# Local attention normalised two steps behind its scores, weight splits held back behind named instructions, projections spread from step 16

## The chip, the core and the metric

The kernel runs on one core of a Trainium2 chip. The metric is the device time of one execution in microseconds. The core has five engines that each take their instructions in order: TensorE (PE; its weight loads are PEld), VectorE (DVE), ScalarE (ACT), GpSimd (POOL) and SyncE (SP), which only issues transfers.

## What is computed

Three layers, one after the other, on 4 batches of 512 local and 32 global rows each (576 in all later), with a width of 512.

```python
# 1 local + global attention, 8 heads of 64, window 32
s_g = scale * q_g @ concat(k_g, k_l).T;  out_g = softmax(s_g) @ concat(v_g, v_l)
s_l = concat(scale * q_l @ k_g.T, where(|i - j| <= 32, scale * q_l @ k_l.T, -1e9))
out_l = softmax(s_l) @ concat(v_g, v_l)
x = rows(concat(out_g, out_l))
# 2 four experts, causal attention, weighted by the two best of x @ w_gate
ye = softmax(causal(scale * (x @ wq[e]) @ (x @ wk[e]).T)) @ (x @ wv[e]) @ wo[e]
x = sum over e of gate_e * ye
# 3 MLP on x and the row before it
k = max((mu_k * x + (1 - mu_k) * x_prev) @ w_k, 0)
out = sigmoid((mu_r * x + (1 - mu_r) * x_prev) @ w_r) * ((k * k) @ w_v)
```

Products that need more than one pass of reduced precision are made of three: a tensor is split into a high part H and a low part L = x - H, and H H, L H and H L are summed (lines 93 to 95).

## The kernel before

**Stage A, local attention.** Thirty-two steps n, four to each of eight groups u. `a_qk` computes scores S on TensorE (L198), VectorE adds the mask `band` and takes the negative maximum (L208, mn), and ScalarE makes the exponentials in place (sm, L211, with their sums su). `a_norm` makes 1/su on VectorE (rc, L223 and 224) and multiplies on GpSimd (pn, L228, and glob, L231). `a_tp` transposes pn on TensorE (pT, L243) and copies it to pt. Once a group `g_qk`, `g_norm`, `g_tp` do the global rows (Sga, pg, mng, pTG), and `a_pv` multiplies by v (x, L311). In the loop over n, `a_norm` does step n-1 and `a_tp` step n-2. `ts` of step n and `pn` have three buffers each (`csm0`, `csm1`).

**Weights of the projections.** `load_wb(step)` issues the transfers of wq, wk or wv (rawwq, ...) at n = 4, 8, 12; `split_wb`, one chunk a step from the same step on, makes H on ScalarE (L154, behind the last exponential) and L on GpSimd (L155).

**Stage B and C, projections and experts.** `b_groups(b)` is a list of projection pieces of batch b; those of batch 0 are laid into steps n = 26 to 33, the others into `c_step`. `c_step(m)` runs 36 units and starts at n = 34: `c_qk` (scores C, csm), `c_norm` (crc; csm on GpSimd, L479), `c_tp` (cT, cpt) and `c_pv` (y), a step apart each; `wo_groups` makes po. The rows of x are cast to H by VectorE (L343).

**Weights of the MLP.** `load_wd` loads a chunk of w_k, w_v or w_r (raw data of 64-bit numbers, taken as pairs of 32-bit words) and splits it at once: Sign and Abs on ScalarE (L125, 126; wg, wy), a maximum on GpSimd (L127), a shift, an or and an xor on VectorE (L129 to 131), H on ScalarE (L132), L on GpSimd (L133). Chunks of w_k come at m = 8, 11, ..., four of w_v at m = 31, 33, 35, 37, the rest of w_v (4 to 7) and w_r behind the last unit.

**Stage D, the MLP.** Nine tiles of tokens. `d_mix` makes the mixed rows (mmr on VectorE, m0, m1 split by ScalarE and GpSimd, L634 and 635), `d_k` k (ksr, k2r, kk; the low part on GpSimd, L651), `d_v` v, `d_r` r, `d_out` the product and its store. For tile 0 TensorE needs all eight chunks of w_v.

**What sets the order.** The code is written as one stream; the framework then orders each engine's instructions by a timeline of its own. `tc.issue_after(i)` around an instruction keeps it behind i. A buffer of a tag is handed out again when its last reader is done.

## Time and profile before

| | us |
|---|---|
| median of 3 runs (lowest, highest) | 583.22 (581.43, 584.19) |
| profiled execution | 579.51 |
| its span | 577.7 |
| TensorE busy, idle in the span | 546.5, 31.2 |
| VectorE, ScalarE, GpSimd busy | 350.3, 330.8, 315.0 |
| granted clock of TensorE, mean | .982 |

The profile gives, for one execution, the busy time of each engine, the idle time before an instruction with the instruction that ended it (its releaser), and the clock that TensorE was granted (1.00 is full, .50 half). An idle time of TensorE is read by following its releaser back: to the engine that was late, and to what that one waited for.

### The profile page before, as it was taken

The page shows a single profiled execution, that of the slowest core. Times are in us where ns is not written, and L with a number is a line of the kernel's source. Part 1 is how long each engine was busy: PE and PEld are TensorE (multiplying, and loading weights), DVE is VectorE, ACT ScalarE, POOL GpSimd, SP SyncE. Part 2 cuts the span into 40 slices and gives each one's busy share as a digit, 9 for nine tenths or more (in the row PEclk, how much of TensorE's full clock was granted, in tenths as well). Part 3 has the DMA queues.
Part 4 walks back from the last instruction along what each step waited for, and adds up shares of the span by engine and source line. Part 5 has one row for each costly group of instructions (what it writes and reads, how often), then busy time and mean ns, then how long its engine had stood idle before and what let it go on. Part 6 is the DMA issues. An engine that isn't in the chain of part 4 may idle for free.

```text
span 577.7 us, 12767 instructions
## 1 busy us (share of the span) xinstructions
PE 546.5 (95%) x4670; PEld 456.8 (79%) x4670; DVE 350.3 (61%) x1145; ACT 330.8 (57%) x995; POOL 315.0 (55%) x416
## 2 busy tenths in 40 slices
PE   3879999999999999799899898999999999999997
PEld 2657767889987888588778786888898989898896
DVE  2545677468678668648788989969343343324211
ACT  3676777555546465347579667677444554434221
POOL 1755765465356546636567999967444444334120
PEclk9897999999999999799999999999999999999999
DMA  8974645023101101011111222010000000000000
GB/s 346 324 210 135 199 172 174 2 76 83 48 1 38 38 21 54 2 37 38 37 38 38 74 74 75 35 39 36 1 38 1 37 1 36 19 19 37 2 19 36
DMA packets 19775, 38.85 MB, mean 67 GB/s; under 512 B 9472, under 2 KB 10496, under 8 KB 19712
## 3 DMA queue, kind: packets, MB, share of 16 engines
q1 hardware_dynamic: 19136, 37.46, 19.9%
q8 instruction: 37, 0.61, 0.4%
q10 hardware_dynamic: 576, 0.57, 0.3%
q14 instruction: 26, 0.21, 0.1%
HBM read 33.57 MB, written 4.46 MB: 66 GB/s over the span
## 4 chain that ended last, share of the span: by engine, by line
PE 65%; DVE 13%; ACT 8%; POOL 5%; DMA 5%; issue 3%; SPq 1%; ACTq 0%; DVEq 0%; POOLq 0%
PE v L93 4%; PE v L94 4%; PE v L95 4%; PE k L94 4%; PE k L93 4%; PE k L95 4%; PE y L557 4%; PE cT L487 3%; PE C L101 3%; PE x L311 3%; PE r L93 2%; DVE x L343 2%; PE r L94 2%; PE r L95 2%; PE S L198 2%
## 5 line engine op out<-in xcount | busy, mean ns | idle before, releaser
L651 POOL TENSOR_TENSOR kk<-k2r,kk 128x256 fp32r<-128x256 f32 x64 | 50.6, 793 | 68.3 <-ACT kk L650 68.3
L648 DVE TENSOR_TENSOR k2r<-ksr 128x256 f32<-128x256 f32 x64 | 36.9, 578 | 70.5 <-ACT ksr L647 64.3
L479 POOL TENSOR_TENSOR csm<-csm,crc 128x128 f32<-128x128 f32 (+3 forms) x64 | 50.1, 803 | 47.3 <-DVE crc L476 22.6
L211 ACT ACTIVATE sm<-sm,mn 128x160 f32<-128x160 f32 x128 | 53.4, 419 | 23.4 <-DVE mn L208 23.1
L631 DVE SCALAR_TENSOR_TENSOR mmr<-xT,mu,mtr 128x256 f32<-128x256 f32 (+4 forms) x96 | 58.8, 648 | 10.7 <-POOL m L635 4.1
L228 POOL TENSOR_TENSOR pn<-sm,rc 128x256 f32<-128x256 f32 x64 | 38.0, 614 | 43.6 <-DVE rc L224 23.2
L463 ACT ACTIVATE csm<-csm,cmn 128x128 f32<-128x128 f32 (+3 forms) x64 | 35.8, 561 | 27.3 <-DVE cmn L461 27.3
L647 ACT ACTIVATE ksr<-k 128x256 f32<-128x256 f32 x64 | 24.1, 377 | 40.5 <-PE k L95 40.0
L630 ACT ACTIVATE mtr<-xT,omu 128x256 f32<-128x256 f32 (+4 forms) x96 | 40.3, 442 | 7.7 <-DVE mmr L631 7.0
L208 DVE CUSTOM_DVE_ANT_0 sm<-S,band 128x160 f32<-128x160 f32 x128 | 34.2, 320 | 16.9 <-DMA band<-in_band_dram 9.0
L635 POOL TENSOR_TENSOR m1L<-mmr,m1H 128x256 fp32r<-128x256 f32 (+1 forms) x36 | 27.6, 779 | 30.5 <-ACT m1H L634 30.4
L650 ACT CAST kk<-k2r 128x256 fp32r<-128x256 f32 x64 | 25.9, 404 | 25.7 <-DVE k2r L648 22.7
L198 PE MATMUL S<-kq 64*64 64x160 f32 x512 | 31.1, 325 | 7.6 <-DMA kq<-in_kq_dram 4.1
L557 PE MATMUL y<-cpt,vC 128*64 128x128 f32 (+1 forms) x320 | 35.8, 300 | 0.0
L461 DVE CUSTOM_DVE_ANT_0 csm<-C,causal 128x128 f32<-128x128 f32 (+3 forms) x64 | 29.7, 485 | 4.9 <-PE C L101 3.5
L696 DVE TENSOR_TENSOR o<-v,rt 128x512 f32<-128x512 f32 x17 | 11.6, 685 | 33.4 <-ACT m1H L634 18.2
L487 PE MATMUL cT<-ident,csm 128*128 128x128 f32 x160 | 27.0, 286 | 5.0 <-DVE cpt L492 2.4
L198 PEld LDWEIGHTS S<-kq 64*64 64x64 f32 x512 | 19.7, 140 | 15.1 <-issue 6.9
L311 PE MATMUL x<-pt,vw 128*64 128x64 f32 x512 | 30.6, 244 | 0.1
L243 PE MATMUL pT<-ident,pn 128*128 128x128 f32 x128 | 22.3, 300 | 8.1 <-DVE mng L274 4.0
L311 PEld LDWEIGHTS x<-pt,vw 128*64 128x64 f32 x512 | 25.9, 149 | 5.0 <-issue 3.9
L557 PEld LDWEIGHTS y<-cpt,vC 128*64 128x64 f32 x320 | 21.7, 137 | 9.1 <-issue 5.7
(408 smaller groups left out, 1894.7 us busy)
## 6 DMA issues: line engine op xcount, KB each, us to landing
kq<-in_kq_dram SPq DMA_DIRECT2D x15, 688.0 KB, 5.5
...
```

The lines of the kernel that those rows point to most:

```text
L93: nc.tensor.matmul(o, wH, xH, start=start, stop=False)
L94: nc.tensor.matmul(o, wH, xL, start=False, stop=False)
L95: nc.tensor.matmul(o, wL, xH, start=False, stop=stop)
L198: nc.tensor.matmul(st[h][64 * c:64 * c + 64, i * W:(i + 1) * W], t[rr, 64 * blk:64 * blk + 64], t[rr, KT0 + 96 * blk:KT0 + 96 * blk + W], ...
L211: last_act = nc.scalar.activation(ts[:, h, i], ts[:, h, i], AF.Exp, bias=mn[:, c:c + 1], scale=-1.0, accum_out=su[:, c:c + 1])
L311: nc.tensor.matmul(xs[pp][rr, 64 * blk:64 * blk + 64], w, pt[:, 2 * pp + m // 2, 2 * h + m % 2, 64 * c:64 * c + 64], start=blk == 0, stop= ...
L479: nc.gpsimd.tensor_tensor(t[:, :w], t[:, :w], rc[:, e:e + 1].to_broadcast([128, w]), op=ALU.mult)
L487: nc.tensor.transpose(pT[:, j * 128:(j + 1) * 128], ts[e][:, j * 128:(j + 1) * 128], ident)
L557: nc.tensor.matmul(yp[64 * e:64 * e + 64, o0:o0 + n], vC[b][:, j, hh * HD:(hh + 1) * HD], pt[:, e, j, 0:n], start=j == 0, stop=j == i and ...
L630: nc.scalar.mul(mt[:, cc], xp, omu[:, kind, c:c + 1])
L631: nc.vector.scalar_tensor_tensor(mm[:, cc], x, mu[:, kind, c:c + 1], mt[:, cc], op0=ALU.mult, op1=ALU.add)
L651: nc.gpsimd.tensor_sub(hl[1], k2, v32(hl[0]))
```

## The change

- `a_norm` runs two steps behind `a_qk`, `a_tp` three; the global parts and `a_pv` move back with them by about a step; the loop gets two steps more. `sm`, `pn`, `csm` and the outputs share one tag of six buffers; `pt` of even groups lies in buffers of `cpt`.
- The first transfers are cut otherwise: the first piece of kq has 448 columns in place of 480, two of the three parts of `band` follow it on SP's queue, the third goes last on ScalarE's.
- wq, wk and wv are loaded at n = 3, 7, 11; their splits run two steps later, two chunks a step, the low parts one step after the high parts and behind the last normalising on GpSimd.
- The projections of batch 0 are spread over n = 16 to 32, and `c_step` starts at n = 33.
- `load_wd` only issues the transfer; the split waits in `pending` until the next load, and its instructions stand behind the last exponential, the last normalising and the last reduction or gate product (`last_act`, `last_pool`, `last_dve`). `split_wo` runs at m = 7.
- The mask `tail` has 32 columns in place of 272, with a third reduction in `l_qk`.

```diff
...
-WB, WS = 4, 4
+WB, WS, WL = 3, 4, 2
...
-B0, CS = 26, 34
+B0, CS = 16, 33
...
-    BUFS = {"W0": 1, "W1": 1, "W2": 1, "x": 1, "qk": 3, "kp": 4, "raw": 2, "wy": 2, "wg": 2, "csm0": 3, "csm1": 3,
+    BUFS = {"W0": 1, "W1": 1, "W2": 1, "x": 1, "qk": 3, "kp": 4, "raw": 2, "wy": 2, "wg": 2, "csm": 6,
             "cpt": 2, "vC": 2, "y": 2, "wo": 2, "pl": 1, "ptl": 1, "rep": 2, "ql": 1}
...
     def load_wd(name, src, c, k, f0):
+        raw = T("raw", [512, 2], f"wraw{name}{c}{k}", U32)
+        nc.sync.dma_start(raw.rearrange("p a b -> p (a b)"),
+                          src.bitcast(U32)[c * 128:(c + 1) * 128, 2 * f0:2 * f0 + 1024])
+        return lambda: split_wd(name, raw, c, k)
+    def split_wd(name, raw, c, k):
         if (name, k) not in wd:
             wd[name, k] = []
             for s, tag in zip("HL", WD_TAG[name, k]):
...
         H_, L_ = [t[c % 4] for t in wd[name, k]]
-        raw = T("raw", [512, 2], f"wraw{name}{c}{k}", U32)
-        nc.sync.dma_start(raw.rearrange("p a b -> p (a b)"),
-                          src.bitcast(U32)[c * 128:(c + 1) * 128, 2 * f0:2 * f0 + 1024])
         lo, hi, hf = raw[:, :, 0], raw[:, :, 1], v32(raw)[:, :, 1]
         y = T("wy", [512], f"wy{name}{c}{k}", U32)
         g = T("wg", [512], f"wg{name}{c}{k}", U32)
-        nc.scalar.activation(v32(g), hf, AF.Sign, bias=tcol)
-        nc.scalar.activation(v32(y), hf, AF.Abs)
-        nc.gpsimd.tensor_scalar(v32(y), v32(y), TINY, None, op0=ALU.max)
-        with tc.issue_after(last_dve.ins) if last_dve else ExitStack():
+        with after(last_act):
+            nc.scalar.activation(v32(g), hf, AF.Sign, bias=tcol)
+            nc.scalar.activation(v32(y), hf, AF.Abs)
+        with after(last_pool):
+            nc.gpsimd.tensor_scalar(v32(y), v32(y), TINY, None, op0=ALU.max)
+        with after(last_dve):
             nc.vector.tensor_scalar(y, y, 3, 0x7fffffff, op0=ALU.logical_shift_left, op1=ALU.bitwise_and)
         nc.vector.scalar_tensor_tensor(g, lo, 29, g, op0=ALU.logical_shift_right, op1=ALU.bitwise_or)
         nc.vector.scalar_tensor_tensor(y, y, 0x7f800000, g, op0=ALU.bitwise_xor, op1=ALU.bitwise_xor)
...
-        with tc.issue_after(last_act.ins):
+        with after(last_act):
             nc.scalar.copy(H_, r)
-        nc.gpsimd.tensor_sub(L_, r, v32(H_))
+        return lambda: nc.gpsimd.tensor_sub(L_, r, v32(H_))
...
-    def load_pair(P, parts=1):
+    def load_pair(P, first=False):
         t = T("kp", [NQ], f"kq{P}")
-        if parts == 1:
+        if not first:
             nc.sync.dma_start(t, kq[P])
         else:
-            for eng, a, b in ((nc.sync, KT0, KT0 + 480), (nc.scalar, 0, 256), (nc.sync, KT0 + 480, NQ),
-                              (nc.scalar, 256, 512)):
-                eng.dma_start(t[:, a:b], kq[P][:, a:b])
+            nc.sync.dma_start(t[:, KT0:KT0 + 448], kq[P][:, KT0:KT0 + 448])
+            nc.scalar.dma_start(t[:, 0:256], kq[P][:, 0:256])
+            nc.sync.dma_start(band[:, 0:2], c_band[:, 0:2])
+            nc.scalar.dma_start(t[:, 256:512], kq[P][:, 256:512])
+            nc.sync.dma_start(t[:, KT0 + 448:], kq[P][:, KT0 + 448:])
+            nc.scalar.dma_start(ident, c_ident)
+            nc.scalar.dma_start(band[:, 2:3], c_band[:, 2:3])
         kqs[P] = t
...
-        ts = T("csm0", [2, 2, W], f"sm{n}")
+        ts = T("csm", [2, 2, W], f"sm{n}")
...
-        o = T("csm1", [4, 2, 64], f"pn{n}")
+        o = T("csm", [4, 2, 64], f"pn{n}")
...
     def a_tp(n):
         u, r = divmod(n, 4)
         if r == 0:
-            pts[u] = T("qk", [4, 4, 128], f"pt{u}")
+            if u % 2:
+                t = T("qk", [4, 4, 128], f"pt{u}")
+                pts[u] = [t[:, j] for j in range(4)]
+            else:
+                ts = [T("cpt", [2, 4, 128], f"pt{u}{j}") for j in range(2)]
+                pts[u] = [t[:, j] for t in ts for j in range(2)]
...
     def load_wo():
         raw = T("raw", [2, DM], "rawwo")
         nc.sync.dma_start(raw, wo.rearrange("(a e) d m -> (e d) a m", a=2))
-        nc.scalar.copy(woS[0], raw)
-        nc.gpsimd.tensor_sub(woS[1], raw, v32(woS[0]))
+        wraw["o"] = raw
+    def split_wo():
+        with after(last_act):
+            nc.scalar.copy(woS[0], wraw["o"])
+        with after(last_pool):
+            nc.gpsimd.tensor_sub(woS[1], wraw["o"], v32(woS[0]))
...
         mn = T("lmn", [4], f"lmn{b}", F32, 1)
         su = T("lsu", [1], f"lsu{b}", F32, 1)
-        nc.vector.tensor_tensor_reduce(out=t[:, 0:HALF], in0=s0[:, :HALF], in1=zcol.to_broadcast([128, HALF]), op0=ALU.add,
-                                       op1=ALU.min, scale=-SCALE, scalar=BIG, accum_out=mn[:, 0:1])
-        nc.vector.tensor_tensor_reduce(out=t[:, HALF:S], in0=s1[:, :HALF], in1=tail, op0=ALU.add, op1=ALU.min,
-                                       scale=-SCALE, scalar=BIG, accum_out=mn[:, 1:2])
-        nc.vector.tensor_tensor(mn[:, 2:3], mn[:, 0:1], mn[:, 1:2], op=ALU.min)
-        nc.scalar.activation(t[:, 0:S], t[:, 0:S], AF.Exp, bias=mn[:, 2:3], scale=-1.0, accum_out=su)
+        for c, (src, o0, m) in enumerate(((s0[:, :HALF], 0, zcol), (s1[:, :HALF - SG], HALF, zcol),
+                                          (s1[:, HALF - SG:HALF], SL, tail))):
+            n = src.shape[1]
+            nc.vector.tensor_tensor_reduce(out=t[:, o0:o0 + n], in0=src, in1=m if m is tail else m.to_broadcast([128, n]),
+                                           op0=ALU.add, op1=ALU.min, scale=-SCALE, scalar=BIG, accum_out=mn[:, c:c + 1])
+        nc.vector.tensor_reduce(mn[:, 3:4], mn[:, 0:3], AX.X, ALU.min)
+        nc.scalar.activation(t[:, 0:S], t[:, 0:S], AF.Exp, bias=mn[:, 3:4], scale=-1.0, accum_out=su)
...
-    load_pair(0, 4)
-    nc.scalar.dma_start(ident, c_ident)
-    nc.scalar.dma_start(band, c_band)
+    load_pair(0, True)
     load_pair(1)
     load_v(0)
     load_v(1)
+    load_pair(2)
     nc.sync.dma_start(vgb, vgd.rearrange("p (u c) -> p u c", u=NG))
-    load_pair(2)
     load_pair(3)
...
             d_k(0, m - K0)
+        if m == 7:
+            split_wo()
         if V0 <= m < V0 + 4 * VS and (m - V0) % VS == 0:
             c = (m - V0) // VS
-            load_wd("v", w_v, c, c // 4, 0)
-        if m >= 8 and (m - 8) % 3 == 0 and (m - 8) // 3 < 8:
-            k = (m - 8) // 3
-            load_wd("k", w_k, k % 4, k // 4, 512 * (k // 4))
+            pending.append(load_wd("v", w_v, c, c // 4, 0))
+        if m >= 7 and (m - 7) % 3 == 0 and (m - 7) // 3 < 8:
+            k = (m - 7) // 3
+            pending.append(load_wd("k", w_k, k % 4, k // 4, 512 * (k // 4)))
+        if len(pending) > 1 or m >= V0 + 4 * VS - 1:
+            for g in pending[:1]:
+                g()
+            del pending[:1]
     fill = b_groups(0)
-    for n in range(NU + 4):
-        if n == 10:
+    NFILL = len(fill)
+    pending = []
+    low = []
+    for n in range(NU + 6):
...
-            nc.vector.tensor_scalar(omu, mu, -1.0, 1.0, op0=ALU.mult, op1=ALU.add)
+        if n == 14:
             ql = T("ql", [2, 2, 128], "ql", F32R)
             qld = [[ql[:, p, s] for s in range(2)] for p in range(2)]
-            nc.gpsimd.memset(v32(ql), 0.0)
+            with after(last_pool):
+                nc.gpsimd.memset(v32(ql), 0.0)
+            with after(last_dve):
+                nc.vector.tensor_scalar(omu, mu, -1.0, 1.0, op0=ALU.mult, op1=ALU.add)
+        u, r = divmod(n, 4)
+        with after(last_pool):
+            for g in low:
+                g()
+        low = []
         if n < NU:
             a_qk(n)
-        if n < NU and n % 4 == 1:
-            g_qk(n // 4)
-        if 0 <= n - 1 < NU:
-            a_norm(n - 1)
-        if n % 4 == 2 and n < NU:
-            g_norm(n // 4)
+        if r == 1 and n < NU:
+            g_qk(u)
         if 0 <= n - 2 < NU:
-            a_tp(n - 2)
-        if n % 4 == 3 and n < NU:
-            g_tp(n // 4)
-        if n % 4 == 1 and n >= 5:
-            a_tg((n - 5) // 4)
-        if n % 4 == 2 and n >= 6:
-            a_pv((n - 6) // 4)
-        if n % 4 == 1 and n // 4 + 1 < NG:
+            a_norm(n - 2)
+        if r == 3 and n < NU:
+            g_norm(u)
+        if 0 <= n - 3 < NU:
+            a_tp(n - 3)
+        if r == 0 and 0 < u <= NG:
+            g_tp(u - 1)
+        if r == 2 and 0 < u <= NG:
+            a_tg(u - 1)
+        if r == 3 and 0 < u <= NG:
+            a_pv(u - 1)
+        if r == 1 and u + 1 < NG:
             for P in range(2):
-                load_v(2 * (n // 4 + 1) + P)
-        if n % 4 == 3 and n // 4 + 2 < NG:
+                load_v(2 * (u + 1) + P)
+        if r == 3 and u + 2 < NG:
             for P in range(2):
-                load_pair(2 * (n // 4 + 2) + P)
+                load_pair(2 * (u + 2) + P)
         if n >= WB and n < WB + 3 * WS:
             step, c = divmod(n - WB, WS)
             if c == 0:
                 load_wb(step)
-            if c < NC:
-                split_wb(step, c)
+            if c >= WL:
+                low += [split_wb(step, 2 * (c - WL) + j) for j in range(2)]
         if B0 <= n < CS:
-            k = -(-len(fill) // (CS - n))
+            k = NFILL * (n + 1 - B0) // (CS - B0) - NFILL * (n - B0) // (CS - B0)
             for g in fill[:k]:
                 g()
             del fill[:k]
...
-        if n == NU + 3:
+        if n == NU + 4:
             pl = T("pl", [640], "pl")
             last_rows()
...
     load_wo()
-    for m in range(max(0, NU + 4 - CS), NCU + 3):
+    for m in range(NU + 6 - CS, NCU + 3):
         c_step(m)
     for g in wo_groups(B - 1):
         g()
+    for g in pending:
+        g()
     for c in range(4, NF):
-        load_wd("v", w_v, c, c // 4, 0)
+        load_wd("v", w_v, c, c // 4, 0)()
     for c in range(NC):
-        load_wd("r", w_r, c, 0, 0)
+        load_wd("r", w_r, c, 0, 0)()
```

How it moves instructions is shown at three places.

Around the weight split of wk in local attention, on ScalarE. Before (sm9 are the exponentials of step 9):

```order
L154 CAST wk_560<-rawwk_561 128x256
L211 ACTIVATE sm9_578,su9_580<-sm9_578,mn9_579 128x160 x4
L154 CAST wk_560<-rawwk_561 128x256
L277 ACTIVATE pg0_90,sug2_600<-pg0_90,mng2_599 128x544
L211 ACTIVATE sm10_651,su10_653<-sm10_651,mn10_652 128x160 x3
L246 COPY pt2_673<-pT8_674 128x512
```

After:

```order
L293 ACTIVATE pg0_90,sug2_593<-pg0_90,mng2_592 128x544
L222 ACTIVATE sm10_629,su10_631<-sm10_629,mn10_630 128x160 x4
L163 CAST wk_512<-rawwk_513 128x256 x2
L222 ACTIVATE sm11_675,su11_677<-sm11_675,mn11_676 128x160 x4
L262 COPY pt20_697<-pT8_699 128x512
L340 COPY xT0_81<-x10_706 128x512
```

The casts of wk stood one by one ahead of, between and behind the exponentials of steps 9 to 11; now two stand together behind those of step 10. On VectorE, steps 4 and 5 (rc is the sum and reciprocal, ISA the reduction or the reading of its result), before:

```order
L208 ISA sm4_280,mn4_281<-S4_1_271,band_68 128x160
L208 ISA mn4_281 128x1
L223 TENSOR_SCALAR rc4_350<-su4_282 128x4
L224 RECIPROCAL rc4_350<-rc4_350 128x4
L208 ISA sm5_322,mn5_323<-S5_0_312,band_68 128x160
L208 ISA mn5_323 128x1
```

After:

```order
L219 ISA sm4_266,mn4_267<-S4_1_257,band_68 128x160
L219 ISA mn4_267 128x1
L264 COPY pt00_238<-pT1_284 128x512
L235 TENSOR_SCALAR rc4_385<-su4_268 128x4
L313 COPY plg_92<-pTh0_296 32x128
L236 RECIPROCAL rc4_385<-rc4_385 128x4
L219 ISA sm5_315,mn5_316<-S5_0_305,band_68 128x160
```

The reciprocal of step 4 stands between the reductions of steps 4 and 5 in both; a copy to pt has come ahead of it.

On GpSimd from the last normalising of stage C (csm3130 and csm3131) on, before (wyv30 is chunk 3 of w_v, half 0):

```order
L479 TENSOR_TENSOR csm3121_4745<-csm3121_4745,crc312_4807 128x384
L127 TENSOR_SCALAR wyv30_4917<-wyv30_4917 128x512
L651 TENSOR_TENSOR kk_4630<-k2r_4629,kk_4630 128x256
L133 TENSOR_TENSOR wv0L0_4557<-wyv20_4844,wv0H0_4556 128x512
L479 TENSOR_TENSOR csm3130_4801<-csm3130_4801,crc313_4854 128x512
L479 TENSOR_TENSOR csm3131_4804<-csm3131_4804,crc313_4854 128x512
L651 TENSOR_TENSOR kk_4630<-k2r_4629,kk_4630 128x256
L496 COPY cpt313_4892<-ptl3_4608 128x4x32 x2
L127 TENSOR_SCALAR wyv41_5008<-wyv41_5008 128x512
L651 TENSOR_TENSOR kk_4630<-k2r_4629,kk_4630 128x256
L133 TENSOR_TENSOR wv0L0_4557<-wyv30_4917,wv0H0_4556 128x512
L651 TENSOR_TENSOR kk_4630<-k2r_4629,kk_4630 128x256
```

After:

```order
L519 COPY cpt313_4891<-ptl3_4605 128x4x32 x2
L501 TENSOR_TENSOR csm3130_4800<-csm3130_4800,crc313_4853 128x512
L501 TENSOR_TENSOR csm3131_4803<-csm3131_4803,crc313_4853 128x512
L136 TENSOR_SCALAR wyv10_4843<-wyv10_4843 128x512
L136 TENSOR_SCALAR wyv20_4916<-wyv20_4916 128x512
L675 TENSOR_TENSOR kk_4627<-k2r_4626,kk_4627 128x256 x2
L142 TENSOR_TENSOR wv0L0_4720<-wyv10_4843,wv0H0_4719 128x512
L659 TENSOR_TENSOR m1L0_4646<-mmr_4624,m1H0_4645 128x256 x2
L142 TENSOR_TENSOR wv0L0_4720<-wyv20_4916,wv0H0_4719 128x512
L136 TENSOR_SCALAR wyv30_4939<-wyv30_4939 128x512
L659 TENSOR_TENSOR m1L0_4646<-mmr_4624,m1H0_4645 128x256 x2
```

The maxima of chunks 1 to 3 (wyv10, wyv20, wyv30) and the low parts made of them stand behind the last csm now; before, only the low part of wyv30 did.

On TensorE at the last v of token tile 0 (v00, v01), before:

```order
L93 MATMUL v00_5105<-wv1H0_5004,kk_4630 128x512
L93 MATMUL v01_5106<-wv1H0_5004,kk_4630 128x512
L93 MATMUL k11_5314<-m0H1_5107,wk0H0_2912 128x256
L94 MATMUL k11_5314<-m0L1_5108,wk0H0_2912 128x256
L95 MATMUL k11_5314<-m0H1_5107,wk0L0_2913 128x256
L93 MATMUL k12_5382<-m0H1_5107,wk0H0_2912 128x256
L94 MATMUL k12_5382<-m0L1_5108,wk0H0_2912 128x256
L95 MATMUL k12_5382<-m0H1_5107,wk0L0_2913 128x256
L93 MATMUL k12_5382<-m0H1_5107,wk0H0_2912 128x256
L94 MATMUL v00_5105<-wv1L0_5005,kk_4630 128x512
L94 MATMUL v01_5106<-wv1L0_5005,kk_4630 128x512
```

After:

```order
L95 MATMUL v00_5114<-wv1H0_5015,kk_4627 128x512
L94 MATMUL v01_5115<-wv1L0_5016,kk_4627 128x512
L95 MATMUL v01_5115<-wv1H0_5015,kk_4627 128x512
L93 MATMUL v00_5114<-wv1H0_5015,kk_4627 128x512
L93 MATMUL v01_5115<-wv1H0_5015,kk_4627 128x512
L94 MATMUL v00_5114<-wv1L0_5016,kk_4627 128x512
L95 MATMUL v00_5114<-wv1H0_5015,kk_4627 128x512
L94 MATMUL v01_5115<-wv1L0_5016,kk_4627 128x512
L95 MATMUL v01_5115<-wv1H0_5015,kk_4627 128x512
L93 MATMUL r00_5256<-wr0H0_5065,m1H0_4645 128x512
L93 MATMUL r01_5277<-wr0H0_5065,m1H0_4645 128x512
L93 MATMUL k10_5306<-m0H1_5116,wk0H0_3062 128x256
```

Before, k of the next tile (k11, k12) stood between these v; now the v stand in a row, and k10 comes behind them.

## Rows read from the trace of the kernel before

**Rows 1.** Busy time of the engines, first part of the page.

```profile
PE 546.5 (95%) x4670; PEld 456.8 (79%) x4670; DVE 350.3 (61%) x1145; ACT 330.8 (57%) x995; POOL 315.0 (55%) x416
```

**Rows 2.** Timeline of TensorE, 0 to 28 us; columns: start, us, engine line op, idle before.

```profile
4.08 2.41 PE L198 MATMUL S<-kq 64*64 64x160 f32 x32 [4.08 <-DMA kq<-in_kq_dram]
...
11.00 1.01 PE L198 MATMUL S<-kq 64*64 64x160 f32 x16 [2.20 <-DVE mn L208]
14.60 1.11 PE L243 MATMUL pT<-ident,pn 128*128 128x128 f32 x4 [2.59 <-POOL pn L228]
...
27.38 0.63 PE L243 MATMUL pT<-ident,pn 128*128 128x128 f32 x4 [1.49 <-DVE rc L223]
```

**Rows 3.** Waits in total; DMA issues of 0 to 16 us: KB, us to landing.

```profile
DVE sm L208 <- DMA band<-in_band_dram: 9.0, 1, 9.0
...
kq<-in_kq_dram SPq DMA_DIRECT2D x1, 240.0 KB, 3.1
band<-in_band_dram ACTq DMA_DIRECT2D x1, 240.0 KB, 7.8
```

**Rows 4.** Stretches: length, busy us (instructions) PE PEld DVE ACT POOL, clock, DMA, GB/s.

```profile
12.00:20.00 8.00, 5.41 (x48) 3.98 (x51) 5.25 (x35) 6.52 (x30) 5.67 (x11) 0.57 1.09 358
44.00:52.00 8.00, 7.80 (x118) 6.60 (x118) 3.38 (x21) 3.86 (x14) 5.20 (x9) 0.62 0.27 81
52.00:160.00 108.00, 106.58 (x1472) 85.37 (x1466) 74.19 (x375) 72.14 (x258) 59.00 (x95) 1.00 0.36 113
232.00:240.00 8.00, 4.36 (x24) 2.92 (x22) 5.85 (x15) 2.28 (x9) 5.31 (x8) 0.65 0.00 0
326.40:357.00 30.60, 27.66 (x181) 23.64 (x182) 27.40 (x33) 20.93 (x49) 29.30 (x27) 1.00 0.26 86
```

**Rows 5.** Timelines of VectorE, ScalarE and TensorE, 26 to 44 us; L155 by line.

```profile
26.46 0.17 DVE L765 TENSOR_SCALAR omu<-mu 128x8 f32<-128x8 f32 x1 [1.48 <-DMA mu<-in_moe_mu_r_dram]
...
41.19 0.40 ACT L154 CAST wk<-rawwk 128x256 fp32r<-128x256 f32 x1 [2.91 <-DMA rawwk<-in_moe_wk_dram]
...
44.20 1.09 PE L243 MATMUL pT<-ident,pn 128*128 128x128 f32 x4 [4.04 <-DVE mng L274]
...
L155 POOL TENSOR_TENSOR wk<-rawwk,wk 128x256 fp32r<-128x256 f32 x4 | 2.9, 727 | 8.6 <-ACT wk L154 8.6
```

**Rows 6.** Timeline of TensorE, 232 to 237 us.

```profile
233.80 0.36 PE L93 MATMUL pv<-wv,x 128*128 128x260 f32 x1 [1.77 <-DVE x L343]
...
236.55 0.87 PE L487 MATMUL cT<-ident,csm 128*128 128x128 f32 x3 [1.88 <-DVE cpt L492]
```

**Rows 7.** Timeline of GpSimd, 323 to 357 us: last csm, last low part of w_v.

```profile
323.71 2.66 POOL L479 TENSOR_TENSOR csm<-csm,crc 128x512 f32<-128x512 f32 x2
...
355.05 1.74 POOL L133 TENSOR_TENSOR wv1L<-wyv,wv1H 128x512 fp32r<-128x512 f32 x1
```

**Rows 8.** By line, 326 to 357 us (busy us, mean ns); the last of the page.

```profile
L127 POOL TENSOR_SCALAR wyv<-wyv 128x512 f32<-128x512 f32 x4 | 6.3, 1590 | 0.0
L133 POOL TENSOR_TENSOR wv1L<-wyv,wv1H 128x512 fp32r<-128x512 f32 x4 | 6.2, 1561 | 1.3 <-ACT wv1H L132 1.3
...
L635 POOL TENSOR_TENSOR m0L<-mmr,m0H 128x256 fp32r<-128x256 f32 x4 | 4.1, 1054 | 0.0
...
L631 DVE SCALAR_TENSOR_TENSOR mmr<-xT,mu,mtr 128x256 f32<-128x256 f32 x8 | 8.3, 1070 | 0.4 <-POOL m1L L635 0.4
...
L631 DVE SCALAR_TENSOR_TENSOR mmr<-xT,mu,mtr 128x256 f32<-128x256 f32 (+4 forms) x96 | 58.8, 648 | 10.7 <-POOL m L635 4.1
```

**Rows 9.** Timeline of TensorE: two k and two v at their pitch.

```profile
348.61 0.28 PE L94 MATMUL k<-m,wk1H 128*128 128x256 f32 x1
348.73 0.28 PE L95 MATMUL k<-m,wk1L 128*128 128x256 f32 x1
...
352.79 0.40 PE L93 MATMUL v<-wv1H,kk 128*128 128x512 f32 x1
353.02 0.40 PE L94 MATMUL v<-wv1L,kk 128*128 128x512 f32 x1
```

46 lines of the change are left out of this document (25 added, 21 removed).

## The prediction

> **What bounds the kernel now.** I read the busy table first, then the idle times of TensorE in the timeline, because TensorE is busy for 546.5 of 577.7 us and a change can gain only in the other 31.2 us and in stretches at a lowered clock [rows 1]. The profiled execution took 579.51 us, 1.8 more than its span; the median of the runs is 583.22, 3.7 above it. I sum against the profiled execution and add 3.7 at the end.
>
> TensorE's idle time has four places. In each the reader is to see who releases TensorE.
> - Start of local attention: 4.08 us for the first kq piece, then 2.20, 2.59 and 1.49 us for VectorE and GpSimd [rows 2]. Behind those three stands one fact: VectorE's first score reduction waited 9.0 us for the mask `band`, which took 7.8 us to land while the first kq piece took 3.1 on SP's queue [rows 3]. The clock is granted at .57 from 12 to 20 us [rows 4], between its levels of 1.2 and 2.4 GHz, much of the stretch at the lower, right after these gaps.
> - 40 to 44 us: ScalarE waited 2.91 us for rawwk with a weight split that stood ahead of the exponentials of step 9; VectorE's reciprocal had to wait for these, and TensorE waited 4.04 us for VectorE [rows 5]. From 44 to 52 us the clock is .62 [rows 4].
> - 233 to 237 us: 1.77 and 1.88 us for VectorE, first for its casts of x [rows 6].
> - Start of the final MLP, 326 to 357 us: GpSimd is busy for 29.30 and VectorE for 27.40 of 30.60 us, TensorE for 27.66 [rows 4]. Here GpSimd sets the pace: it finishes the last `csm` of the attention at 326.4 and the last low part of w_v at 356.8 [rows 7], almost without a pause.
>
> From 52 us to the end of the attention TensorE is otherwise nearly always busy, so a lead won early is carried along, until something else is late.
>
> **The change part by part.**
>
> *First loads.* Two thirds of `band` (160 KB) move to SP's queue right behind the first kq piece. The first piece took 3.1 us for 240 KB and `band` 7.8 [rows 3]; at the 358 GB/s of 12 to 20 us [rows 4] 160 KB more is half a microsecond. I let `band` land at 4.6 to 5.0 and VectorE start at 5 instead of 10.04. TensorE does not gain these 5 us: it still waits for kq, and then for a chain of four reductions, four exponentials and the normalising. Of the 2.20 + 2.59 + 1.49 = 6.3 us of idle I take about half away, 3.3; the bounds are 2.5 (about one of the gaps) and 5 (the whole lead of VectorE).
> The Trainium skill speaks against the queue as the reason (DMA: Bandwidth & Descriptors, section "Issuing engines are not separate DMA queues"): transfers of all queues run on the same engines and interleave. By that rule only the bytes ahead of `band` count; the sum stays as it is if these are fewer, and the first gain goes to its lower bound if the split of kq makes up for it.
>
> *omu.* It waited 1.48 us for mu [rows 5] and now stands at step 14; its cover is that mu was requested nine steps earlier. That gain is within the 3.3.
>
> *Weights of the projections.* They are loaded at steps 3, 7 and 11, and split two steps later, behind the exponentials of the step. The order of ScalarE shows the wk splits now behind the exponentials of step 10, where the first stood ahead of those of step 9, and rawwk is requested a step earlier. I take the whole stall of 4.04 us away, and of the clock of .62 on 8 us, which is work lost against full clock (8 x .38 = 3.0 us of the higher clock not granted), 3.0. What is late next: GpSimd now has two low parts of wk in a row (727 ns each [rows 5], so 1.5) ahead of the normalising of step 8, and the same at step 12. I charge 1 us for both together, from 0 (hidden behind the extra step that the pipeline now has) to 3. Local attention so gains 3.3 + 4.0 + 3.0 - 1 = **9.3 us**, 7 to 13.
>
> *Normalising two steps behind.* No instruction is added. On VectorE the sum and reciprocal of a step still stand right behind the reductions of the same step and ahead of those of the next, so the wait for the exponentials is not gone everywhere. What it gains is in the 9.3; I cost the deeper pipeline at nothing more. One shared set of six buffers in place of three and three, pt in other buffers: nothing either, with -1 to +2 for a buffer that comes free late.
>
> *Projections of batch 0 from step 16.* The same work is spread over 17 steps instead of 8. TensorE was busy for 106.58 of the 108 us from 52 to 160 [rows 4], so spreading gains nothing there: 0, with -1 to +2 for the seam to the attention.
>
> *Short tail.* Eight VectorE instructions fewer in all, where TensorE has its work: 0.
>
> *Splits of w_k, w_v held back.* A chunk's GpSimd maximum, VectorE shifts and subtraction are issued one load later, each behind what is then last on its engine. Two effects.
> At 233 us less split work stands ahead of the casts, and the gap of 3.65 us with its clock of .65 over 8 us (2 to 3 us more) may shrink. I take 3 of that 6; bounds 6 gained and 2 lost, since the same work must stand somewhere.
> At the start of the MLP, the order of GpSimd shows three chunks of w_v behind the last `csm` that were partly done by then before. From the last `csm` to the last low part of w_v stood 5 maxima, 5 low parts, 6 kk, 8 m and two short copies; now 8 maxima, 7 low parts, 6 kk and 12 m. At the mean durations there (1.59 a maximum, 1.56 a low part, 1.05 an m [rows 8]; the copies I count as one m) the difference is 3 x 1.59 + 2 x 1.56 + 3 x 1.05 = 11.0 us, on 29.3 busy [rows 4]: 40 us. With each instruction a tenth shorter it would be 36. Meanwhile TensorE has less to do: before, three k groups of the next token tile stood between the last v of tile 0; now these v stand in a row, and k10 behind them. Ahead of the last v are left 48 k at a pitch of .12 us (5.7), 48 v at .23 (11.2) [rows 9], 48 po (272 columns to k's 256, so about .125 each, 6.0) and some y, an estimated 1 us: 24 us. TensorE so waits 40 - 24 = 16 us, where it waited 30.60 - 27.66 = 2.9. That is 13.1 more, of which a little comes back where GpSimd then has fewer splits left. I take **12**: 7 with shorter instructions and more of the k work ahead, 17 if a stretch of lowered clock follows as after 44 us.
> The Trainium skill says why GpSimd may be longer still (SBUF — State Buffer, section "SBUF: two separate sides"): VectorE and GpSimd share one pair of ports, held for a whole instruction. The trace agrees in kind: the mmr of VectorE take 1070 ns each in this stretch [rows 8] and 648 over the whole run [rows 8]. By it the three VectorE steps of each chunk would come on top, and 12 would be nearer 17.
>
> Sum: -9.3 - 3 + 12 = -.3 us; 579.5 - .3 + 3.7 = **582.9 us**.
>
> **The rivals.**
> 1. *The wait at the MLP is hidden, and the gain of local attention is kept.* For it: the attention's end comes 12 us earlier, GpSimd is busy for only 55% of the span [rows 1], and if it ran the first maxima of w_v before its last `csm`, the queue behind would be shorter. Against it: their order is fixed behind it. With a cost of 4 (the present 2.9 and a little): -9.3 - 3 + 4 = -8.3, 574.9 us.
> 2. *The queue at the MLP costs its upper price and GpSimd's low parts delay step 8 and 12.* GpSimd becomes the bound in both places: -7 + 0 + 17 = +10, 593 us. It decides as soon as the stretch from the last `csm` to the last low part of w_v is longer than about 42 us while local attention gains less than 7.
> 3. *The step behind does nothing.* VectorE's reciprocal of a step stands ahead of the reductions of the next one, as before, and waits for ScalarE each time; only the first loads gain. -3.3 - 2 + 12 = +6.7, 590 us. Against it: the wait of 4.04 us had a DMA as its cause, and that is gone in any order.
>
> **How the numbers follow.** The forecast (about given back, 577.5 to 588) has a chance of .45, rival 1 .25, rival 2 .15, rival 3 .15. Half a per cent, about what a measurement of this kernel can tell from no change, is 2.9 us, so the bounds are 580.3 and 586.1. Of the forecast's .45 I put .13 under, .22 within and .10 above; rival 1 is faster with all its .25, rival 2 slower with all its .15, rival 3 slower with .10 and within with .05. Faster .38, same .27, slower .35. Both signs hold most of the chance, so the forecast's own range is 577.5 to 588; the range for 8 in 10 reaches to rival 1 and almost to rival 2: 573.5 to 592.
>
> **What would show it.** VectorE's first reduction at 5 us; no wait of ScalarE for rawwk; the scores of step 20 on TensorE some 9 us earlier than before; the last `csm` on GpSimd about 12 us earlier than 326.4; from there 40 us to the last low part of w_v, and TensorE idle for about 16 us among the v of tile 0. I am wrong if that stretch is near 30 us (then faster, rival 1), if the lead at step 20 is under 7 us (rivals 2, 3), or if a new wait appears between 160 and 320 us, where I put none.

## The result, and the profile after

The changed kernel takes 588.31 us (median, 588.06 to 589.68), the kernel before 582.33 (581.10 to 584.19) beside it: a ratio of 1.0105, with a 95% interval of 1.007 to 1.014. It is slower by about 1%. The prediction was 582.9, with 573.5 to 592 as its range: the time lies inside, but the forecast of no change was wrong. The profiled execution took 588.06 us with a span of 586.3, 8.6 more than the 577.7 of before.

The first fence has the busy line of the page and busy time by stretch (columns as in [rows 4]): the first 140 us, the seam to the expert attention, the gap at 228 us and the clock behind it, and the time from the last `csm` to the last low part of w_v.

```profile
PE 551.9 (94%) x4670; PEld 458.9 (78%) x4670; DVE 342.2 (58%) x1153; ACT 331.1 (56%) x995; POOL 315.6 (54%) x416
...
0.00:140.00 140.00, 130.78 (x1889) 99.79 (x1890) 88.06 (x483) 93.86 (x349) 78.02 (x139) 0.99 0.53 170
140.00:180.00 40.00, 37.16 (x298) 31.25 (x294) 27.95 (x126) 20.26 (x62) 18.25 (x24) 0.96 0.04 14
...
228.05:240.00 11.95, 11.95 (x60) 9.13 (x61) 5.62 (x23) 4.87 (x15) 5.23 (x10) 0.59 0.05 11
320.30:361.20 40.90, 28.42 (x164) 22.61 (x164) 35.27 (x42) 26.76 (x65) 39.62 (x35) 0.87 0.28 84
...
0.00:140.00 140.00, 123.79 (x1748) 93.95 (x1749) 82.98 (x462) 92.16 (x342) 76.74 (x133) 0.95 0.54 175
```

The last line is the kernel before over its first 140 us. TensorE is idle there for 16.2 us before and 9.2 after, at a clock of .95 and .99. The second fence has TensorE's gaps in the changed kernel in order of time, and with them VectorE's first reduction and GpSimd's last `csm` and last low part of w_v.

```profile
5.40 0.32 DVE L219 CUSTOM_DVE_ANT_0 sm<-S,band 128x160 f32<-128x160 f32 x1 [4.40 <-PE S L209]
...
15.10 0.65 PE L259 MATMUL pT<-ident,pn 128*128 128x128 f32 x4 [3.95 <-POOL pn L240]
...
56.79 0.77 PE L209 MATMUL S<-kq 64*64 64x160 f32 x16
...
66.92 0.76 PE L198 MATMUL S<-kq 64*64 64x160 f32 x8
...
154.76 0.37 PE L459 MATMUL gl<-gb,rsel 128*128 128x16 f32 x2 [1.85 <-DVE crc L496]
...
228.05 0.88 PE L510 MATMUL cT<-ident,csm 128*128 128x128 f32 x3 [2.32 <-DVE cpt L515]
...
318.08 2.22 POOL L501 TENSOR_TENSOR csm<-csm,crc 128x512 f32<-128x512 f32 x2
...
346.77 0.95 PE L93 MATMUL v<-wv1H,kk 128*128 128x512 f32 x2 [3.45 <-ACT wv1H L141]
350.72 0.80 PE L94 MATMUL v<-wv1L,kk 128*128 128x512 f32 x1 [3.00 <-POOL wv1L L142]
...
359.31 1.22 PE L93 MATMUL v<-wv1H,kk 128*128 128x512 f32 x2 [3.18 <-ACT wv1H L141]
...
359.92 1.27 POOL L142 TENSOR_TENSOR wv1L<-wyv,wv1H 128x512 fp32r<-128x512 f32 x1
```

The two rows of scores, at 56.79 after and at 66.92 before, are both step 16 (256 score matmuls stand ahead): local attention leads by 10.1 us. At step 20, which the prediction named as a sign, the lead is 8.8 (72.60 against 81.37). The last `csm` ends at 320.30, against 326.37 [rows 7]: of the lead 6.1 us are left. From there to the last low part of w_v (361.19) are 40.9 us, against 30.4, and TensorE is busy for 28.42 of them. From the last `csm` to the end are 266.0 us, against 251.3: 14.7 more. So 6.1 - 14.7 = -8.6.

| | last csm ends | to last low part of w_v | from last csm to the end | time | ratio (95%) |
|---|---|---|---|---|---|
| before | 326.4 | 30.4 | 251.3 | 582.3 | 1 |
| changed | 320.3 | 40.9 | 266.0 | 588.3 | 1.0105 (1.007 to 1.014) |
| a1, splits at the load | 326.1 | 23.6 | 253.2 | 579.2 | .9956 (.9929 to .9984) |
| a2, no maximum on GpSimd | 319.7 | 31.2 | 256.5 | 577.6 | .9899 (.9865 to .9934) |
| b1, before + held splits | 328.2 | 40.9 | 265.9 | 594.7 | 1.0198 (1.0166 to 1.023) |
| c1, w_v early | 326.0 | 23.1 | 252.5 | 581.7 | .9998 (.9979 to 1.0016) |
| a3, projections late | 322.8 | 40.9 | 266.6 | 588.3 | 1.0112 (1.0066 to 1.0158) |
| a5, experts from step 35 | 317.9 | 40.9 | 266.8 | 588.1 | 1.0108 (1.0078 to 1.0138) |
| c2, a1 and a5 | 323.1 | 23.6 | 253.2 | 577.1 | .992 (.9895 to .9945) |
| a4, one step behind | 325.1 | 41.0 | 266.0 | 594.1 | 1.0224 (1.0182 to 1.0266) |
| a6, loads of before | 320.9 | 40.9 | 266.6 | 589.8 | 1.0139 (1.0109 to 1.0169) |
| b2, before + first loads | 343.4 | 30.4 | 251.4 | 596.3 | 1.0232 (1.0205 to 1.0258) |
| b3, b2 + omu | 337.8 | 30.4 | 251.5 | 594.2 | 1.0206 (1.0173 to 1.0239) |
| b5, before + weights, omu | 323.0 | 30.4 | 251.4 | 577.4 | .992 (.9886 to .9954) |

The first three columns are read from each run's profiled execution (GpSimd's timeline and the span), the last two are medians of the timed runs and their ratio to the kernel before, run on the same chip. Behind each row of the first columns stands a single execution. Seven of these kernels have the same code up to step 16 (the changed one, a1, a2, a3, a5, c1 and c2), and the scores of step 16 come at 56.8 to 60.0 us in them; a difference of 2 or 3 us in the first column is to be read with that.

### The profile page after: what moved, and what is told of

The parts are those of the page before. It is cut to its first block, busy times and chain, and to the rows that moved or that the text cites. A ratio compares the mean times of both kernels' runs of the same rounds, so it can differ in the third digit from the quotient of the medians.

```text
span 586.3 us, 12786 instructions
## 1 busy us (share of the span) xinstructions
PE 551.9 (94%) x4670; PEld 458.9 (78%) x4670; DVE 342.2 (58%) x1153; ACT 331.1 (56%) x995; POOL 315.6 (54%) x416
## 5 line engine op out<-in xcount | busy, mean ns | idle before, releaser
L672 DVE TENSOR_TENSOR k2r<-ksr 128x256 f32<-128x256 f32 x64 | 34.4, 537 | 78.5 <-ACT ksr L671 74.6
L501 POOL TENSOR_TENSOR csm<-csm,crc 128x128 f32<-128x128 f32 (+3 forms) x64 | 48.7, 781 | 45.7 <-DVE crc L498 14.5
L655 DVE SCALAR_TENSOR_TENSOR mmr<-xT,mu,mtr 128x256 f32<-128x256 f32 (+4 forms) x96 | 52.0, 581 | 14.2 <-POOL m1L L659 6.5
L209 PE MATMUL S<-kq 64*64 64x160 f32 x512 | 32.3, 323 | 4.3 <-DMA kq<-in_kq_dram 4.0
L93 PE MATMUL v<-wv1H,kk 128*128 128x512 f32 x68 | 27.4, 415 | 6.9 <-ACT wv1H L141 6.9
L510 PE MATMUL cT<-ident,csm 128*128 128x128 f32 x160 | 29.0, 295 | 4.7 <-DVE cpt L515 2.3
L94 PE MATMUL v<-wv1L,kk 128*128 128x512 f32 x68 | 28.1, 413 | 5.5 <-POOL wv1L L142 5.5
L244 POOL TENSOR_TENSOR glob<-sm,rc 128x128 f32<-128x128 f32 x32 | 13.0, 406 | 37.4 <-DVE rc L236 26.0
L365 POOL TENSOR_TENSOR x<-xT,x 128x256 fp32r<-128x256 f32 (+1 forms) x32 | 24.0, 777 | 11.9 <-DVE x L364 11.9
```

The source lines that it names most:

```text
L93: nc.tensor.matmul(o, wH, xH, start=start, stop=False)
L94: nc.tensor.matmul(o, wH, xL, start=False, stop=False)
L501: last_pool = nc.gpsimd.tensor_tensor(t[:, :w], t[:, :w], rc[:, e:e + 1].to_broadcast([128, w]), op=ALU.mult)
L655: nc.vector.scalar_tensor_tensor(mm[:, cc], x, mu[:, kind, c:c + 1], mt[:, cc], op0=ALU.mult, op1=ALU.add)
L672: nc.vector.tensor_mul(k2, s, s)
```

## The experiments on the splits held back

**a1: the splits at the load.** In the changed kernel:

```diff
-        with after(last_act):
-            nc.scalar.activation(v32(g), hf, AF.Sign, bias=tcol)
-            nc.scalar.activation(v32(y), hf, AF.Abs)
-        with after(last_pool):
-            nc.gpsimd.tensor_scalar(v32(y), v32(y), TINY, None, op0=ALU.max)
+        nc.scalar.activation(v32(g), hf, AF.Sign, bias=tcol)
+        nc.scalar.activation(v32(y), hf, AF.Abs)
+        nc.gpsimd.tensor_scalar(v32(y), v32(y), TINY, None, op0=ALU.max)
...
-            pending.append(load_wd("v", w_v, c, c // 4, 0))
+            load_wd("v", w_v, c, c // 4, 0)()
```

and the same for w_k.

> The changed kernel, with the splits of w_k and w_v issued at the load and without the fences on ScalarE and GpSimd, as before; all else as changed. Theory (the splits held back fill GpSimd's queue behind the last csm): its order now has 5 maxima, 5 low parts, 2 kk and 6 m from the last csm to the last low part of w_v, in place of 8, 7, 6 and 12, so that stretch falls from 40.9 us to about 25 to 30, TensorE's idle time in it from 13.6 us to under 5, and the time from 588.3 to about 575. Rival (the MLP's start is late for another reason, such as VectorE, or the attention's parts work against each other): the stretch stays at 38 us or more and the time at 585 or more.

Measured: 579.2 us. The stretch fell to 23.6 us and the rest of the kernel to 253.2, 12.8 us less, as the theory has it. But the last `csm` came at 326.1 and not at 320.3: 5.8 us of the gain were paid in the attention. Busy time from the last `csm` on and behind the first new gap, VectorE's work ahead of that gap, and TensorE's two gaps:

```profile
326.10:349.80 23.70, 21.19 (x148) 18.86 (x148) 20.87 (x23) 16.30 (x39) 23.70 (x20) 1.00 0.31 104
180.00:200.00 20.00, 19.54 (x128) 16.04 (x129) 11.53 (x39) 9.42 (x26) 11.32 (x15) 0.75 0.18 53
...
175.12 1.99 DVE L137 SCALAR_TENSOR_TENSOR wgk<-wrawk,wgk 128x512 uint32<-128x512 uint32 x1
...
177.37 2.62 DVE L362 CAST x<-xT 128x256 fp32r<-128x256 f32 x4
...
178.53 0.36 PE L93 MATMUL pv<-wv,x 128*128 128x260 f32 x1 [1.69 <-DVE x L362]
...
180.46 0.88 PE L508 MATMUL cT<-ident,csm 128*128 128x128 f32 x3 [1.09 <-DVE cpt L513]
```

VectorE does a split step of w_k (wgk, 1.99 us) right ahead of the casts of x for which TensorE waits; TensorE loses 1.69 + 1.09 us, and the clock is .75 over the next 20 us, 5 us of the higher clock not granted. So the split work costs wherever it stands: some 6 us among the units of the attention, 13 to 15 behind them.

**b1: the held splits alone.** The kernel before with `split_wd`, `pending`, the three fences and w_k from m = 7, as in the change's diff, and nothing else of it.

> The kernel before, with only the held-back splits of w_k and w_v added (pending, and the fences on ScalarE and GpSimd; w_k from step 7). Theory: GpSimd's queue behind the last csm becomes that of the changed kernel (8 maxima, 7 low parts, 6 kk, 12 m), the stretch 40 us as there against 30.4, and the time 582.3 + 13 = 595. Rival (the queue costs only in company with the earlier end of the attention): at most 586.

Measured: 594.7 us, with the theory's numbers. Busy time of the stretch:

```profile
328.20:369.10 40.90, 28.27 (x164) 22.57 (x164) 35.29 (x42) 26.74 (x65) 39.62 (x35) 0.87 0.27 83
```

GpSimd is busy for 39.62 of 40.90 us, the same as in the changed kernel. The rest of the kernel is 265.9 us, as there. The queue's price does not hang on the earlier end of the attention. And the last `csm` came 1.9 us later than before: the held splits won the attention nothing that shows.

**a2: without the maximum.** The changed kernel, GpSimd's maximum left out for w_v and w_r.

```diff
-        with after(last_pool):
-            nc.gpsimd.tensor_scalar(v32(y), v32(y), TINY, None, op0=ALU.max)
+        if name == "k":
+            with after(last_pool):
+                nc.gpsimd.tensor_scalar(v32(y), v32(y), TINY, None, op0=ALU.max)
```

> The changed kernel without the maximum on GpSimd for the chunks of w_v and w_r (the lower bound on absolute values is left out for them). Theory (GpSimd paces the start of the MLP): 8 maxima of 1.6 us leave the stretch, which falls from 40.9 to about 29 us, and the time from 588.3 to about 577. Rival (VectorE paces it with its three steps per chunk): the stretch stays at 36 us or more, with VectorE busy for 95% of it, and the time at 584 or more.

Measured: 577.6 us, and a stretch of 31.2.

```profile
319.70:350.90 31.20, 26.50 (x168) 21.76 (x168) 31.10 (x37) 23.27 (x54) 26.73 (x24) 0.92 0.40 128
```

The time is the theory's, and the stretch is 9.7 us shorter with 12.9 us less of GpSimd's work in it. The row also shows what is late next: VectorE is busy for 31.10 of 31.20 us, GpSimd for 26.73. GpSimd paced the changed kernel; VectorE comes next, 9.7 us earlier.

**c1: w_v early.** The changed kernel with w_k held back, but w_v split at its load, without the two fences, and V0 = 28 in place of 31; what is left of w_k is split from step 30 on in place of 38.

> The changed kernel with the splits of w_k held back as in the change, but those of w_v issued at the load, without the fences on ScalarE and GpSimd, and three steps earlier (steps 28, 30, 32, 34). Theory (GpSimd has room ahead of the last csm and none behind it): its order has 5 maxima, 5 low parts, 2 kk and 6 m behind the last csm, about 24 us; the last csm stays near 320 to 322 us and the time is 572 to 575. Rival (split work standing in the attention costs there what it saves behind, as in the run with all splits at once): 578 or more.

Measured: 581.7 us, not told apart from the kernel before. The queue behind the last `csm` became as short as expected (23.1 us), but the last `csm` came at 326.0: the rival was right. At 284 us c1 still led the changed kernel by 1.4 us, so the loss lies behind that, where the splits of w_v now stand. A stretch there, and TensorE's wait at its end:

```profile
290.00:300.00 10.00, 8.47 (x54) 5.77 (x52) 9.97 (x23) 10.00 (x27) 9.51 (x8) 1.00 0.33 105
...
300.51 0.59 PE L93 MATMUL po<-ytH,woH 128*128 128x272 f32 x1 [1.50 <-DVE cpt L515]
```

VectorE, ScalarE and GpSimd are all nearly full, and at the last units TensorE waits .73, 1.93 and .53 us for GpSimd's `csm`, in the changed kernel .24, .44 and .53. With a1 this says that GpSimd's idle time ahead of the last `csm` is no room for this work: it needs VectorE and ScalarE too, and the `csm` come later.

## The experiments on the seam and the projections

**a3: projections late.** In the changed kernel `B0, CS = 26, 33`.

> The changed kernel with the projections of batch 0 in steps 26 to 32 again (B0 = 26) and not 16 to 32. Theory of the prediction (spreading is worth nothing, the stall at 152 to 155 us belongs to the rows of the global part that come in there): within 2 us of 588.3, the stall of 1.85 us for crc and the half clock after it stay. Rival (projections done early leave TensorE without other work at the seam): the stall goes and the time is 584 or less.

Measured: 588.3 us, the stall at the seam unchanged (1.84 us for crc). Spreading the projections is worth nothing that these runs (584.7 to 591.2 us) can tell.

**a5: expert attention from step 35.** In the changed kernel `B0, CS = 16, 35`.

> The changed kernel with the expert attention starting at step 35 and not 33, so that its first global unit comes two steps behind the values and gates of the global rows, as before. In TensorE's order 45 projection matmuls more then stand between the last pvl and gl. Theory (the stall of 2.3 us at 152 to 155 us and the lowered clock after it come from the gate chain of VectorE standing right ahead of gl): the stall is under .5 us, the last csm at about 316 us in place of 320.3, and the time is 584. Rival (the wait moves to another unit, or the later start costs as much): 587 or more.

Measured: 588.1 us. In the profile the stall is gone; what is left of gaps between 140 and 230 us:

```profile
154.05 0.39 PE L93 MATMUL pv<-wv,x 128*128 128x260 f32 x1 [0.22 <-DVE cpt L515]
...
176.80 0.52 PE L510 MATMUL cT<-ident,csm 128*128 128x128 f32 x3 [0.52 <-DVE crc L496]
...
227.35 0.88 PE L510 MATMUL cT<-ident,csm 128*128 128x128 f32 x3 [2.32 <-DVE cpt L515]
```

and the last `csm` comes at 317.9, 2.4 us earlier than in the changed kernel. So the place of the stall is shown: VectorE finished the gates of the global rows (gsl, gatel, gb) at 154.6 us, right ahead of `gl` (the profile puts the wait down to the crc that followed); the change starts the experts a step earlier while the values of the global rows come later. Its price to the last `csm` was 2.4 us and not 4. The profiled execution is 1.6 us shorter than the changed kernel's, as the end came .8 us later behind the last `csm`; the medians, 588.1 and 588.3, do not tell the two apart.

**c2: a1 and a5 together.** 

> The changed kernel with both mended: splits issued at the load as before, and the expert attention from step 35. Theory (the two costs are apart and add): 579.2 - 4 = 575, faster than both. Rival (the split work standing in the attention meets the earlier units and makes stalls of its own at 178 and 234 us in any case): 578 or more.

Measured: 577.1 us, .8% faster than before. The last `csm` is 3.0 us earlier than in a1, so the two costs are apart; the gaps at 178 us are those of a1, as the rival has it. The time lies between the theory's 575 and the rival's 578.

## The experiments on local attention

**b2: the first loads alone.** The kernel before with `load_pair(0, True)` of the change, its pieces and their order.

> The kernel before, with only the new first loads (first kq piece of 448 columns, two thirds of band behind it on SP's queue, the third last). Theory of the prediction: VectorE starts at about 5 us and not at 10, TensorE gains about 3.3 us by step 8; time 579. Rival (the wait for rawwk at 41 us and other transfers come at their own time and take the gain back): within 1 us of 582.3, with a longer wait for rawwk.

Measured: 596.3 us, 14 us slower than before: neither theory had that. VectorE's wait for mu, and TensorE's gap behind it:

```profile
29.21 0.17 DVE L767 TENSOR_SCALAR omu<-mu 128x8 f32<-128x8 f32 x1 [6.86 <-DMA mu<-in_moe_mu_r_dram]
...
30.20 1.09 PE L247 MATMUL pT<-ident,pn 128*128 128x128 f32 x4 [6.04 <-DVE mng L278]
...
DVE rc L227 <- ACT sm L215: 37.9, 29, 4.5
```

The framework orders by its own timeline. With `band` early it set another order on VectorE, from the 15th instruction on: the first reciprocals stand ahead of reductions that they followed before, and VectorE waits for ScalarE's exponentials 29 times in place of 18. omu keeps its place in the order, but VectorE reaches it 2.6 us earlier than before, and mu, requested at 23.90 us in place of 21.64, lands later. Until then the kernel was ahead: the scores of step 6 came at 23.39 us, before at 24.63. The last `csm` is 17 us later than before.

**b3: the first loads and omu.** The same with mu at step 5, omu and ql at step 14.

> The kernel before with the new first loads and, besides, omu moved as in the change (mu requested at step 5, omu and the clearing of ql at step 14). In the run of the first loads alone VectorE waited 6.9 us for mu with omu and TensorE 6.0 us behind it. Theory (omu standing early is what turned the first loads into a loss): that wait is gone and the time is 576 to 580. Rival (with one step between scores and normalising the earlier start runs into the transfers of wk and wv and keeps its stalls of 3.7 and 4.5 us): 588 or more.

Measured: 594.2 us, the rival. The wait for mu is 3.9 us now, and the gaps behind the exponentials stay, one of them behind rawwk as before:

```profile
43.67 0.40 ACT L154 CAST wk<-rawwk 128x256 fp32r<-128x256 f32 x1 [2.97 <-DMA rawwk<-in_moe_wk_dram]
...
46.68 1.09 PE L247 MATMUL pT<-ident,pn 128*128 128x128 f32 x4 [4.11 <-DVE mng L278]
...
DVE rc L227 <- ACT sm L215: 38.7, 30, 4.1
```

**a4: one step behind.** In the changed kernel `a_norm(n - 1)` and `a_tp(n - 2)`.

> The changed kernel with the normalising one step and the transposes two steps behind the scores again; all else as changed. Theory (the lead of 10 us comes from the first loads, omu and the weights, not from the step): the scores of step 16 come at 57 to 58 us as in the changed kernel, and the time is within 2 us of 588.3. Rival (the extra step is what hides ScalarE's and GpSimd's work): TensorE waits for pn or for the reciprocal in every group, step 16 comes 4 us later or more, and the time is 592 or more.

Measured: 594.1 us, 5.8 more than the changed kernel; the last `csm` is 4.8 us later. TensorE's gaps for pn in the first groups:

```profile
15.52 0.66 PE L259 MATMUL pT<-ident,pn 128*128 128x128 f32 x4 [2.94 <-POOL pn L240]
...
28.82 0.66 PE L259 MATMUL pT<-ident,pn 128*128 128x128 f32 x4 [2.01 <-POOL pn L240]
...
44.47 1.12 PE L259 MATMUL pT<-ident,pn 128*128 128x128 f32 x4 [2.01 <-POOL pn L240]
```

In the changed kernel the gaps of the second and third of these groups are .48 and .47 us. The scores of step 16 come at 63.1 us, later than in each of the seven runs with the extra step (56.8 to 60.0). The extra step hides the normalising up to GpSimd's pn: the rival.

**a6: the loads of before.** The changed kernel with the old pieces of kq and `band` whole on ScalarE's queue.

> The changed kernel with the first loads of before (kq in the old pieces, band whole on ScalarE's queue). Theory (with the step between scores and normalising the early band is worth its 3.3 us): VectorE starts at 10 us and the time is 591 to 592. Rival (the extra step makes the start indifferent, since TensorE has scores to do meanwhile): within 1 us of 588.3.

Measured: 589.8 us. VectorE starts at 9.00 us in place of 5.40, yet TensorE's gaps in the first 20 us are smaller:

```profile
9.00 0.33 DVE L215 CUSTOM_DVE_ANT_0 sm<-S,band 128x160 f32<-128x160 f32 x1 [8.00 <-DMA band<-in_band_dram]
...
9.96 2.64 PE L205 MATMUL S<-kq 64*64 64x160 f32 x32 [1.28 <-DVE mn L215]
13.91 1.12 PE L255 MATMUL pT<-ident,pn 128*128 128x128 f32 x4 [1.31 <-POOL pn L236]
...
17.30 1.11 PE L255 MATMUL pT<-ident,pn 128*128 128x128 f32 x4 [0.99 <-POOL pn L236]
```

They sum to 3.6 us, and the one gap of the changed kernel at 15.10 is 3.95; in the six other runs with the early `band` and the extra step it is 3.5 to 4.3. With two steps between, TensorE has scores to do while VectorE waits. The scores of step 16 come at 59.2 us, within the 56.8 to 60.0 of those runs, and the last `csm` .6 us later than in the changed kernel. By the medians the early `band` is worth 1.5 us, between theory and rival; the intervals (1.007 to 1.014, 1.0109 to 1.0169) overlap, so neither nothing nor the 3.3 is excluded by the time alone.

**b5: the weights of the projections and omu.** The kernel before with WB = 3, the splits two steps later, `low`, mu at step 5 and omu at step 14.

> The kernel before with the splits of wq, wk and wv two steps after their loads (steps 3, 7, 11), two chunks a step, low parts a step later, and mu requested at step 5 with omu at step 14; first loads, the one step between scores and normalising, and the splits of w_k and w_v as before. Theory of the prediction (the wait for rawwk and the lowered clock after it are worth 4.0 + 3.0 us by themselves): the gap of 4.0 us at 44 us is gone and the time is 575. Rival (with one step between, VectorE stands in front of ScalarE's exponentials in every step, so other gaps take its place): 581 or more.

Measured: 577.4 us, .8% faster than before, and the last `csm` 3.4 us earlier. The gap of 4.04 us at 44 us became:

```profile
41.05 0.63 PE L246 MATMUL pT<-ident,pn 128*128 128x128 f32 x4 [1.15 <-DVE mng L277]
```

The mechanism is the theory's; the size is 4.5 us and not 7, since gaps of 2.01 and 1.58 us at 25 and 63 us came with it.

## Why the prediction was wrong

The mechanism of the largest term, the MLP, was right, and its size too small. What failed is that the attention was to end 12.3 us earlier and ended 6.1 earlier. By terms:

- *First loads, 3.3 us.* The transfers did what was said: VectorE's first reduction came at 5.40 us. The step that failed was to take half of three gaps as VectorE's late start: with the deeper pipeline TensorE's gaps at the start are no smaller with the early `band` than with the late one (a6), and the time shows 1.5 us, not clear of the noise. Alone (b2) the same loads cost 14 us, through the order that they led to, which no gap of the profile could tell.
- *Weights, 4.0 + 3.0 - 1.* Right in kind; b5 has 4.5 us with omu. In the changed kernel ScalarE still waits 1.01 us for rawwk at 36.9 us, but TensorE has no gap behind it.
- *Normalising two steps behind, 0.* Wrong: a4 has 4.8 to 5.8 us. The reciprocal did stay ahead of the next reductions, but TensorE's gap is at pn, behind GpSimd, and that is what the step hides. Together local attention led by 10.1 us at step 16, where the prediction had 9.3: the sum came out by luck, with its terms wrong.
- *Projections from step 16, 0.* Right (a3).
- *Short tail, 0.* VectorE has eight instructions more and not fewer (1153 against 1145 in the busy lines); no run tried this part alone.
- *The seam, not more than 2.* The new stall at 152 to 155 us cost 2.4 us (a5). Between step 16 and the last `csm` the changed kernel lost 4.0 us of its lead, and a5 only 1.1 (9.6 to 8.4). The prediction named the seam but did not count how far the gates stand from `gl`.
- *The gap at 233 us, -3.* It did not come. At 228 us the changed kernel waits 2.32 + .24 us in place of 3.65, but is at .59 of the clock for the 12 us after; and in b1, with the held splits alone, the last `csm` came no earlier. The step that failed is to take the split work ahead of the casts of x for what made the gap. In neither kernel did it hold them up: VectorE had been idle for ScalarE just before, for ql before and for csm after, as the fence shows (its first line is the kernel before). The gap is made by the casts themselves, and these took longer, 4.16 us in place of 3.50 (the casts of before ended at the second gap of [rows 6]), with GpSimd's low part and csm beside them. Four casts of the same size took 2.30 us fifty us earlier, and .89 us at 129.55, where GpSimd was busy beside them for only .5 us:

```profile
232.47 0.18 DVE L372 TENSOR_TENSOR ql<-pb21q,ql 64x32 fp32r<-64x32 f32 x1 [0.18 <-ACT ql L371]
...
129.55 0.89 DVE L364 CAST x<-xT 128x256 fp32r<-128x256 f32 x4
...
174.60 2.30 DVE L364 CAST x<-xT 128x256 fp32r<-128x256 f32 x4 [0.15 <-PE pb11k L95]
...
222.49 0.17 DVE L496 TENSOR_SCALAR crc<-csu 128x2 f32<-128x2 f32 x1 [0.46 <-ACT csm L485]
...
223.41 4.16 DVE L364 CAST x<-xT 128x256 fp32r<-128x256 f32 x4
...
223.34 1.26 POOL L142 TENSOR_TENSOR wk0L<-wyk,wk0H 128x512 fp32r<-128x512 f32 x1 [3.62 <-DVE crc L498]
224.57 2.13 POOL L501 TENSOR_TENSOR csm<-csm,crc 128x512 f32<-128x512 f32 x2
```

  The Trainium skill (SBUF — State Buffer, section "SBUF: two separate sides") gives a reason, ports that VectorE and GpSimd hold in turn. The rows agree in kind. In a1 the low part stands elsewhere: there the casts that the units of 228 us need took 2.58 us, and TensorE waited .18.
- *The start of the MLP, +12.* The mechanism is shown (b1, a1, a2), with its stretch: 40 us were forecast, 40.9 measured. The price was 14.7 us, within the bounds of 7 and 17: TensorE waited 12.5 us in the stretch where 16 were forecast, but the clock fell to .87 over it, with about 4.6 us more of busy time for the same matmuls to the end. The prediction had the clock as a bound of 17 and took the lower value. Of the two means that it set beside each other for VectorE's mmr, 1070 and 648 ns, the second mixes five shapes; the shape 128x256 alone has 831 ns over the whole run of before.

So -9.3 - 3 + 12 = -.3 became -6.1 + 14.7 = +8.6 from span to span: 3 us for the gap at 233, over 2 for the seam and 2.7 at the MLP, where the clock fell, make up most of the 8.9 between them. The first two could have been met: the 3 us were taken as a middle of two bounds with no row for it, and at the seam the gates were not counted. The medians differ by 6.0 and not by 8.6, mostly since the profiled execution of before (579.51) was 2.8 us below its median (582.33).

What stays open: why the early `band` alone leads the framework to an order with more waits (b2, b3) was not tried, nor what a lighter split on VectorE and GpSimd would give. The short tail, `split_wo` at m = 7 and the shared buffers were in no run by themselves.
